# Token-ordered transposed blocks, a one-run load of block 0, an earlier W_out and a split last eviction in a convolution + GELU MLP kernel

## The chip, the cores and the metric

One core of one Trainium2 chip. The metric is the device time of one execution in microseconds (us); lower is better. The kernel before takes 686.33 us (median of 3 executions, 686.15 to 686.39). Inside a profile the clock starts with the span, so a profile's span (684.45 us for the kernel before) is about 1.8 us shorter than the time of the same execution. The pages print spans to 0.1 us; spans to 0.01 us are read from the kept traces. The profile is always that of one execution, the first (for the kernel before one of 686.27 us, which is not among the three); the other executions give only their time.

## The reference

A causal depthwise convolution with 7 taps over tokens (softmax over the taps, one weight row for each of 8 heads), then a two-layer MLP with exact GELU, on 8 x 4096 tokens of 192 values:

```python
w = softmax(weight, axis=-1)                       # [8 heads, 7 taps]
x_pad = concat([zeros(B, 6, 192), x], axis=1)
y[b, s, h, :] = sum_k w[h, k] * x_pad[b, s + k, h, :]
out = gelu(y.reshape(32768, 192) @ w_in) @ w_out   # w_in [192, 2048], w_out [2048, 192]
```

## The kernel before

The tokens are cut into two halves, which run side by side in the upper and the lower 64 partitions, and each half into 35 blocks: 6 of 256 tokens (0 to 5), then 29 of 512, of which the last (34) is evicted and stored in its own way. PE is TensorE, DVE is VectorE, ACT is ScalarE; SP, ACT and GpSimd issue the DMAs. For each block: DMA loads, three DVE transposes of 32x32 tiles (a column of `xT` is then a token), 7 taps on the DVE (blocks 0 and 1 on PE instead, with diagonal matrices), the first matmul (PE), GELU (ACT), the second matmul (PE), an eviction (a copy of the result out of `ob`, the PSUM tensor that the second matmul writes), stores. In the code shown, `...` marks a cut, and comments at the ends of lines are added.

The order of the tokens is set by the load. Partition `s` of a group of 32 takes `mb` *consecutive* tokens; after the transposes column `32*j + s` holds token `s*mb + j`:

```python
def load(e, n, qs=(0, 2, 1, 3), sm=None):
    mb = WS[n] // 32
    ...                                  # q: two halves of the tokens x two halves of the 192 values
        ap(xin[n % NX], 32*q*(TB//32*DQ), [[TB//32*DQ, 32], [DQ, mb], [1, DQ]]),
        ap(xt, off, [[mb * D, 32], [D, mb], [1, DQ]]),        # DQ = 96 values = 384 bytes
```

So a tap, one token back, is a shift by 32 columns, and the first 6*32 columns of each block (the halo) must be filled by GpSimd, mostly from the same block:

```python
src = ap(xT[n % 2], p * XW + 32 * kt, [[NP * XW, 128], [1, w]])      # a tap's source (DVE)
g.tensor_copy(ap(t, 1, [..., [32, HB], [1, 31]]),                    # 558 elements per partition
              ap(t, WS[n], [..., [32, HB], [1, 31]]))                # GpSimd, each block from 2 on
```

At the start GpSimd issues the W_in loads, then ten x loads of blocks 1 to 3 with W_out between them. SP and ACT each issue two of block 0's four loads; ACT does so *ahead of the Exp of the softmax*:

```python
load(a, 0, (2, 3))                 # ACT: two DMA issues
a.wait_ge(S_ACTP, 1)
a.wait_ge(S_PRO, 1)
a.activation(out=wex[:, :], in_=wsb[:, :], func=AF.Exp, ...)
```

At the end each 128x384 result of the last block is evicted by the DVE, and SP and ACT then issue two stores of 48 KB each.

## Time and profile before

| | before |
|---|---|
| time, median of 3 | 686.33 us |
| profile span | 684.45 us |
| busy PE / DVE / ACT / GpSimd | 677.3 / 580.5 / 532.6 / 46.0 us |
| first tap matmul of block 0 | 8.04 us |
| a 512-token block in the steady part | 20.72 us |
| last matmul to end of span | 3.40 us |

How to read it: PE is busy all the time and owns 96% of the chain of work that ended last. An engine with idle time may become faster and nothing happens.

### The profile page before, as it was taken

How to read it: one execution, taken by the hardware profiler on the slowest of the kernel's cores; microseconds unless marked ns; L12 is line 12 of the kernel's file. 1: busy time of each engine (PE TensorE's matmuls, PEld its weight loads, DVE VectorE, ACT ScalarE, POOL GpSimd, SP SyncE). 2: the span in 40 equal slices, each digit the busy share in tenths (PEclk: the TensorE clock that was granted, in tenths of full speed). 3: DMA queues.
4: the chain of work that ended last, by engine and by line, in shares of the span. 5: the costliest groups of instructions: out<-in, count | busy, mean ns of one | idle time of the engine just before them, and what ended most of it. 6: DMA issues, size and time to landing. Idle time of an engine off the chain costs nothing.

```text
span 684.5 us, 27314 instructions
## 1 busy us (share of the span) xinstructions
PE 677.3 (99%) x12548; PEld 409.0 (60%) x12548; DVE 580.5 (85%) x914; ACT 532.6 (78%) x536; POOL 46.0 (7%) x97
## 2 busy tenths in 40 slices
PE   8999999999999999999999999999999999999997
PEld 4899655555555555555555555555555555555556
DVE  7999999888899888898888898888898888998702
ACT  6788987877787777787877878777778777877771
POOL 8110000000000000000000000000000000000000
PEclk9999999999999999999999999999999999999999
DMA  8544531344432344422444422444322444221224
GB/s 135 95 107 99 117 61 32 64 94 95 94 67 50 76 94 95 93 52 55 85 94 95 88 51 53 95 94 95 72 54 66 95 94 95 61 53 31 48 49 94
DMA packets 133234, 53.66 MB, mean 78 GB/s; under 512 B 127552, under 2 KB 132960, under 8 KB 133120
## 3 DMA queue, kind: packets, MB, share of 16 engines
q1 hardware_dynamic: 128144, 48.78, 33.3%
q0 software_dynamic: 3792, 2.56, 2.4%
q8 instruction: 98, 1.61, 1.0%
q10 hardware_dynamic: 1184, 0.59, 0.3%
q14 instruction: 16, 0.13, 0.1%
HBM read 28.31 MB, written 25.17 MB: 78 GB/s over the span
## 4 chain that ended last, share of the span: by engine, by line
PE 96%; ACT 2%; DMA 1%; issue 0%; DVE 0%; SPq 0%
PE hp L683 47%; PE ob L747 42%; PE ob L714 6%; ACT gT L612 2%; PE ob L640 1%; DMA xin<-in_x_dram 1%; ACT osb L227 0%; DVE osb L247 0%; SPq L258 0%; DVE osb L229 0%; DVE xT L478 0%; ACT xTb L572 0%; SPq L795 0%; ACT xc L579 0%
## 5 line engine op out<-in xcount | busy, mean ns | idle before, releaser
L612 ACT ACTIVATE gT<-hp 128x1024 bf16<-128x1024 f32 x512 | 523.4, 1024 | 132.7 <-PE hp L683 129.6
L683 PE MATMUL hp<-xc,win 64*64 64x512 bf16 (+2 forms) x6048 | 418.5, 366 | 1.1 <-ACT gT L612 0.7
L747 PE MATMUL ob<-gT,wout 64*64 64x512 bf16 x5376 | 366.3, 376 | 0.0
L508 DVE SCALAR_TENSOR_TENSOR acc<-xT,wcol,acc 128x512 f32<-128x512 f32 (+1 forms) x495 | 314.0, 697 | 0.0
L683 PEld LDWEIGHTS hp<-xc,win 64*64 64x64 bf16 (+1 forms) x6048 | 187.7, 106 | 135.6 <-ACT gT L612 2.1
L747 PEld LDWEIGHTS ob<-gT,wout 64*64 64x64 bf16 x5376 | 172.1, 118 | 123.0
L247 DVE STREAM_TRANSPOSE osb<-ob 128x512 f32<-128x512 f32 x84 | 73.7, 880 | 86.8 <-PE ob L747 86.8
L478 DVE STREAM_TRANSPOSE xT<-xin 128x512 f32<-128x512 f32 (+1 forms) x105 | 78.5, 799 | 0.2 <-DMA xin<-in_x_dram 0.2
L508 DVE SCALAR_TENSOR_TENSOR xc<-xT,wcol,acc 128x512 bf16<-128x512 f32 (+1 forms) x99 | 65.1, 711 | 0.0
L374 POOL COPY xT<-xT 128x558 f32<-128x558 f32 x33 | 21.6, 654 | 578.6 <-DVE xT L478 578.6
L501 DVE TENSOR_SCALAR acc<-xT,wcol 128x512 f32<-128x512 f32 (+1 forms) x99 | 56.1, 618 | 1.1
L714 PE MATMUL ob<-wout,gT 64*128 64x192 bf16 x1024 | 52.2, 243 | 0.3
L714 PEld LDWEIGHTS ob<-wout,gT 64*128 64x128 bf16 x1024 | 43.5, 94 | 6.5 <-PE ob L714 0.6
L357 POOL COPY xT<-xT 128x18 f32<-128x18 f32 x30 | 11.6, 387 | 1.4 <-DVE xc L461 1.4
L229 DVE COPY osb<-ob 128x384 f32<-128x384 f32 x4 | 2.2, 557 | 7.8 <-PE ob L714 7.8
L625 PE MATMUL hp<-warm 128*128 128x512 bf16 x16 | 5.7, 533 | 1.3 <-DVE warm L394 1.3
L640 PE MATMUL ob<-xTb,dg 64*64 64x256 bf16 x84 | 5.3, 271 | 1.1 <-ACT xTb L572 1.1
L227 ACT ACTIVATE osb<-ob 128x384 f32<-128x384 f32 x12 | 5.8, 486 | 0.0
L258 POOL DMA_DIRECT2D xin<-in_x_dram x10 | 5.8, 588 | 0.0
L640 PEld LDWEIGHTS ob<-xTb,dg 64*64 64x64 bf16 x84 | 4.3, 106 | 2.2 <-ACT xTb L572 1.6
L625 PEld LDWEIGHTS hp<-warm 128*128 128x128 bf16 x16 | 2.0, 129 | 4.5 <-issue 2.7
L324 POOL DMA_DIRECT2D win<-in_moe_w_in_dram x6 | 3.9, 651 | 0.0
(32 smaller groups left out, 21.7 us busy)
## 6 DMA issues: line engine op xcount, KB each, us to landing
xin<-in_x_dram SPq DMA_DIRECT2D x116, 192.0 KB, 4.4
out_dram<-osb SPq DMA_DIRECT2D x112, 192.0 KB, 3.6
out_dram<-osb SPq DMA_DIRECT2D x56, 48.0 KB, 1.7
xin<-in_x_dram SPq DMA_DIRECT2D x12, 96.0 KB, 2.7
xin<-in_x_dram POOLq DMA_DIRECT2D x10, 96.0 KB, 2.7
wout<-in_moe_w_out_dram POOLq DMA_DIRECT2D x1, 768.0 KB, 8.6
win<-in_moe_w_in_dram POOLq DMA_DIRECT2D x4, 96.0 KB, 4.2
win<-in_moe_w_in_dram POOLq DMA_DIRECT2D x2, 192.0 KB, 5.3
```

The source lines that it names most:

```text
L247: v.transpose(ap(osb[m % 2], j, [[8 * C, 128], [C // 2, TB // 32], [NP, 32]]), bank(ring(m, j)),).then_inc(S_EV)
L357: g.tensor_copy(dst, ap(xT[(n - 1) % 2], WS[n - 1] + 31, [[NP * XW, 128], [XW, NP], [32, HB]],),).then_inc(S_HALO)
L374: g.tensor_copy(ap(t, 1, [[NP * tw, 128], [tw, NP], [32, HB], [1, 31]]), ap(t, WS[n], [[NP * tw, 128], [tw, NP], [32, HB], [1, 31]]),).the ...
L478: v.transpose(ap(xT[n % 2], p * XW + HL, [[NP * XW, 128], [1, w]]), ap(xin[n % NX], p, [[TB // 32 * DQ, 128], [DQ, w // 32], [NP, 32]],),) ...
L501: ins = v.tensor_scalar(a, src, wk, None, ALU.mult)
L508: ins = v.scalar_tensor_tensor(dst, src, wk, a, op0=ALU.mult, op1=ALU.add)
L612: a.activation(out=ap(gT[n % 2], i * c * 2 * w, dst), in_=ap(hp[u % 2], 0, src), func=AF.Gelu,).then_inc(S_GELU)
L625: t.matmul(hp[1][:, 0:512], warm[:, 0:128], warm[:, :])
L640: ins = t.matmul(bank(CONVB[n][p], r, w), dg[r, d0 : d0 + 64], xTb[PC[n]][r, x0 : x0 + w], start=(k == KS - 1), stop=(k == 0), tile_positi ...
L683: ins = t.matmul(hp[u % 2][fo : fo + fw, o : o + w], win[r, f1 : f1 + fw], xc[n % 2][r, p * TB : p * TB + w], start=(p == 0), stop=(p == N ...
L714: ins = t.matmul(bank(bb[sub], w=C), gT[m % 2][r, c0 : c0 + 128], wout[r, CH[i] * C : (CH[i] + 1) * C], start=(ph == 0 and i == 0), stop=( ...
L747: ins = t.matmul(bank(ring(m, j), slice(64 * h, 64 * h + 64), w), ap(wout, 64 * hf * NF * C + CH[i] * C + j, [[NF * C, 64], [NP, 64]],), g ...
```

## The change

Its intent: keep tokens in order, so that a tap is a shift by one column and the halo is 6 columns; save GpSimd's long copies; store in token order; load block 0 in one contiguous run per partition; issue W_out before the x loads of the later blocks; halve the last evictions, and store the last results with one larger DMA per queue instead of two. The core of the diff:

```diff
+    HX = 8
+    HF = HX - (KS - 1)
+    XW = HX + TB
...
+                if n == 0:
+                    dst = [[TB // 32 * DQ, 32], [1, mb * D - DQ]]      # one run of 1440 elements
+                    src = [[mb * D, 32], [1, mb * D - DQ]]
+                else:
+                    dst = [[TB // 32 * DQ, 32], [DQ, mb], [1, DQ]]
+                    src = [[D, 32], [32 * D, mb], [1, DQ]]             # tokens 32 apart
...
-                src = ap(xT[n % 2], p * XW + 32 * kt, [[NP * XW, 128], [1, w]])
+                src = ap(xT[n % 2], p * XW + HF + kt, [[NP * XW, 128], [1, w]])
...
             halo(0)
-            load(g, 1, SW[1], S_XG[1])
-            load(g, 2, SW[2], S_XG[2])
             g.dma_start(... wout ...)
             halo(1)
-            load(g, 3, SW[3], S_XG[3])
...
-            load(sp, 1, (0, 1))
-            sp.wait_ge(S_XG[3], 64)
+            load(sp, 1)
+            load(sp, 2)
+            sp.wait_ge(S_WOUT, 16)
+            load(sp, 3)
...
-                store_group(a, NB - 1, g, (2, 3))
+                evac_half(a, g, 1)            # ACT evicts one half, the DVE the other
+                store_half(a, g, 1)           # one store of 96 KB per queue
```

Block 0 alone keeps its old order, because there the one-run load delivers consecutive tokens.

More of the change, by code (lines that the diff above doesn't have):

```diff
@@ L42, in bass_lightweight_conv__then__act_gelu_exact_kernel @@
     assert NF == 16
+    HX = 8
+    HF = HX - (KS - 1)
+    XW = HX + TB
     HB = KS - 1
     HL = 32 * HB
-    XW = HL + TB
     XB = HL + WS[0]
@@ L82, in bass_lightweight_conv__then__act_gelu_exact_kernel @@
         CH += [2 * s, 2 * s + 1, NF // 2 + 2 * s, NF // 2 + 2 * s + 1]
-    PLAIN = [NCH[n] > 1 or n == NB - 1 for n in range(NB)]
     assert all(WS[n] == TB for n in range(M0, NB))
@@ L87, in bass_lightweight_conv__then__act_gelu_exact_kernel @@
     for n in range(NB):
-        OUTS.append((64 * NG[n] if PLAIN[n] else 64) + (OUTS[n - 2] if n >= 2 else 0))
+        k = 64 if n == 0 or M0 <= n < M1 else 16 * NG[n] if n < NB - 1 else 32 * NG[n]
+        OUTS.append(k * (NG[0] if n == 0 else 1) + (OUTS[n - 2] if n >= 2 else 0))
     es = ExitStack()
@@ L128, in bass_lightweight_conv__then__act_gelu_exact_kernel @@
         ob = pst("ob", [128, 2048])
-        SW = {1: (2, 3), 2: (0, 2, 1, 3), 3: (0, 2, 1, 3)}
         S_WSB = sem("S_WSB")
@@ L135, in bass_lightweight_conv__then__act_gelu_exact_kernel @@
         S_WOUT = sem("S_WOUT")
-        S_XG = {n: sem("S_XG%d" % n) for n in SW}
         S_XIN = [sem("S_XIN%d" % i) for i in range(NX)]
@@ L158, in bass_lightweight_conv__then__act_gelu_exact_kernel @@
         S_EVA = sem("S_EVA")
+        S_EVB = sem("S_EVB")
         block = es.enter_context(nc.Block())
@@ L183, in bass_lightweight_conv__then__act_gelu_exact_kernel @@
         for n in range(NB):
-            HC.append(HC[n] + (1 + NP if n in PC else 2))
+            HC.append(HC[n] + (1 + NP if n == 0 else 1))
         def wcols(hf, f):
@@ L190, in xin_at @@
         def xin_at(n):
-            return sum(64 - 16 * len(SW.get(m, ())) for m in range(n % NX, n + 1, NX))
+            return 64 * (n // NX + 1)
         def banks(m, g):
@@ L217, in wait_banks @@
                 t.wait_ge(S_EV, EVC[M1] + (-2 if e == 0 else e - 1))
+                if e >= 2:
+                    t.wait_ge(S_EVB, e - 1)
         def evac(e, m, g):
@@ L225, in evac, with evac_half, store_half @@
             src = ap(ob, 512 * b0, [[2048, 128], [512 * (b1 - b0), 2], [1, C]])
-            if m < NA:
-                e.activation(out=dst, in_=src, func=AF.Copy).then_inc(S_EVA)
-            else:
-                e.tensor_copy(dst, src).then_inc(S_EV)
+            e.activation(out=dst, in_=src, func=AF.Copy).then_inc(S_EVA)
+        def evac_half(e, g, h):
+            m = NB - 1
+            e.wait_ge(S_MM2, MMC[m] + g + 1)
+            if g == 0:
+                e.wait_ge(S_OUT[m % 2], OUTS[m - 2])
+            dst = osb[m % 2][:, (4 * h + g) * C : (4 * h + g + 1) * C]
+            src = bank(banks(m, g)[h], w=C)
+            if h == 0:
+                e.tensor_copy(dst, src).then_inc(S_EV)
+            else:
+                e.activation(out=dst, in_=src, func=AF.Copy).then_inc(S_EVB)
+        def store_half(e, g, h):
+            m = NB - 1
+            if h == 0:
+                wait_ev(e, m, g)
+            else:
+                e.wait_ge(S_EVB, g + 1)
+            e.dma_start(
+                ap(outt, (h * HALF + OFF[m] + 128 * g) * C, [[C, 128], [1, C]]),
+                osb[m % 2][:, (4 * h + g) * C : (4 * h + g + 1) * C],
+            ).then_inc(S_OUT[m % 2], 16)
         UPLO = [(1, 0), (0, 2), (2, 1)]
@@ L257, in load @@
                 off = ((q // 2) * HALF + OFF[n]) * D + DQ * (q % 2)
-                e.dma_start(
-                    ap(
-                        xin[n % NX],
-                        32 * q * (TB // 32 * DQ),
-                        [[TB // 32 * DQ, 32], [DQ, mb], [1, DQ]],
-                    ),
-                    ap(xt, off, [[mb * D, 32], [D, mb], [1, DQ]]),
-                ).then_inc(sm or S_XIN[n % NX], 16)
-        def store_group(e, m, g, qs=(0, 1, 2, 3)):
-            mb = WS[m] // 32
-            wait_ev(e, m, g)
-            for q in qs:
+                if n == 0:
+                    dst = [[TB // 32 * DQ, 32], [1, mb * D - DQ]]
+                    src = [[mb * D, 32], [1, mb * D - DQ]]
+                else:
+                    dst = [[TB // 32 * DQ, 32], [DQ, mb], [1, DQ]]
+                    src = [[D, 32], [32 * D, mb], [1, DQ]]
@@ new lines, in load, with store @@
+                e.dma_start(
+                    ap(xin[n % NX], 32 * q * (TB // 32 * DQ), dst), ap(xt, off, src)
+                ).then_inc(sm or S_XIN[n % NX], 16)
+        def store(e, m):
+            if m < M0:
+                for g in range(NG[m]):
+                    wait_ev(e, m, g)
+                    if m > 0:
+                        e.dma_start(
+                            ap(
+                                outt,
+                                (OFF[m] + 128 * g) * C,
+                                [[C, 128], [HALF * C, 2], [1, C]],
+                            ),
+                            ap(osb[m % 2], g * C, [[8 * C, 128], [4 * C, 2], [1, C]]),
+                        ).then_inc(S_OUT[m % 2], 16)
+                        continue
+                    mb = WS[m] // 32
+                    for q in range(4):
+                        e.dma_start(
+                            ap(
+                                outt,
+                                (OFF[m] + 4 * g + q) * C,
+                                [[mb * C, 32], [HALF * C, 2], [1, C]],
+                            ),
+                            ap(
+                                osb[m % 2],
+                                32 * q * 8 * C + g * C,
+                                [[8 * C, 32], [4 * C, 2], [1, C]],
+                            ),
+                        ).then_inc(S_OUT[m % 2], 16)
+                return
+            wait_ev(e, m, NP - 1)
+            for q in range(4):
@@ L274, in store_group @@
                         outt,
-                        (OFF[m] + 4 * g + q) * C,
-                        [[mb * C, 32], [HALF * C, 2], [1, C]],
+                        ((q // 2) * HALF + OFF[m]) * C + (q % 2) * (C // 2),
+                        [[C, 32], [32 * C, WS[m] // 32], [1, C // 2]],
                     ),
@@ L279, in store_group @@
                         osb[m % 2],
-                        32 * q * 8 * C + g * C,
-                        [[8 * C, 32], [4 * C, 2], [1, C]],
+                        32 * q * 8 * C,
+                        [[8 * C, 32], [C // 2, WS[m] // 32], [1, C // 2]],
                     ),
                 ).then_inc(S_OUT[m % 2], 16)
-        def store(e, m):
-            if PLAIN[m]:
-                for g in range(NG[m]):
-                    store_group(e, m, g)
-                return
-            j = NG[m]
-            mb = WS[m] // 32
-            wait_ev(e, m, EVC[m + 1] - EVC[m] - 1)
-            for q in range(4):
-                if M0 <= m < M1:
-                    dst = ap(
-                        outt,
-                        ((q // 2) * HALF + OFF[m]) * C + (q % 2) * (C // 2),
-                        [[mb * C, 32], [C, mb], [1, C // 2]],
-                    )
-                    src = ap(
-                        osb[m % 2],
-                        32 * q * 8 * C,
-                        [[8 * C, 32], [C // 2, mb], [1, C // 2]],
-                    )
-                else:
-                    dst = ap(
-                        outt,
-                        (OFF[m] + j * q) * C,
-                        [[mb * C, 32], [HALF * C, 2], [1, j * C]],
-                    )
-                    src = ap(
-                        osb[m % 2],
-                        32 * q * 8 * C,
-                        [[8 * C, 32], [4 * C, 2], [1, j * C]],
-                    )
-                e.dma_start(dst, src).then_inc(S_OUT[m % 2], 16)
         @block.gpsimd
@@ L344, in halo @@
             def halo(n):
-                t, tw = (xTb[PC[n]], XB) if n in PC else (xT[n % 2], XW)
-                dst = ap(t, 0, [[NP * tw, 128], [tw, NP], [32, HB]])
-                if n >= 2 and n not in PC:
+                if n == 0:
+                    t = xTb[0]
+                    g.memset(
+                        ap(t, 0, [[NP * XB, 128], [XB, NP], [32, HB]]), 0.0
+                    ).then_inc(S_HALO)
+                    for p in range(NP):
+                        g.wait_ge(S_TR, p + 1)
+                        g.tensor_copy(
+                            ap(t, p * XB + 1, [[NP * XB, 128], [32, HB], [1, 31]]),
+                            ap(
+                                xT[0],
+                                p * XW + HX + WS[0] - HL,
+                                [[NP * XW, 128], [32, HB], [1, 31]],
+                            ),
+                        ).then_inc(S_HALO)
+                    return
+                t, tw = (xTb[1], XB) if n in PC else (xT[n % 2], XW)
+                dst = ap(t, HF, [[NP * tw, 128], [tw, NP], [1, HB]])
+                if n >= 2:
                     if n - 2 in PC:
@@ L354, in halo @@
                     g.memset(dst, 0.0).then_inc(S_HALO)
-                else:
-                    g.wait_ge(S_TR, NP * n)
-                    g.tensor_copy(
-                        dst,
-                        ap(
-                            xT[(n - 1) % 2],
-                            WS[n - 1] + 31,
-                            [[NP * XW, 128], [XW, NP], [32, HB]],
-                        ),
-                    ).then_inc(S_HALO)
-                if n in PC:
-                    for p in range(NP):
-                        g.wait_ge(S_TR, NP * n + p + 1)
-                        g.tensor_copy(
-                            ap(t, p * tw + 1, [[NP * tw, 128], [32, HB], [1, 31]]),
-                            ap(xT[n % 2], p * XW + WS[n], [[NP * XW, 128], [32, HB], [1, 31]]),
-                        ).then_inc(S_HALO)
-                    return
-                g.wait_ge(S_TR, NP * (n + 1))
-                g.tensor_copy(
-                    ap(t, 1, [[NP * tw, 128], [tw, NP], [32, HB], [1, 31]]),
-                    ap(t, WS[n], [[NP * tw, 128], [tw, NP], [32, HB], [1, 31]]),
-                ).then_inc(S_HALO)
+                    return
+                g.wait_ge(S_TR, NP * n)
+                if n == 1:
+                    src = ap(
+                        xT[0],
+                        HX + WS[0] - HL + 31,
+                        [[NP * XW, 128], [XW, NP], [32, HB]],
+                    )
+                else:
+                    src = ap(
+                        xT[(n - 1) % 2],
+                        HF + WS[n - 1],
+                        [[NP * XW, 128], [XW, NP], [1, HB]],
+                    )
+                g.tensor_copy(dst, src).then_inc(S_HALO)
             g.wait_ge(S_IDN, 2)
             halo(0)
-            load(g, 1, SW[1], S_XG[1])
-            load(g, 2, SW[2], S_XG[2])
             g.dma_start(
@@ L454, in cast @@
                 v.tensor_copy(
-                    ap(xTb[PC[n]], p * XB + HL, [[NP * XB, 128], [1, WS[n]]]),
-                    ap(xT[n % 2], p * XW + HL, [[NP * XW, 128], [1, WS[n]]]),
+                    ap(xTb[PC[n]], p * XB + HX, [[NP * XB, 128], [1, WS[n]]]),
+                    ap(xT[n % 2], p * XW + HX, [[NP * XW, 128], [1, WS[n]]]),
                 ).then_inc(S_CAST[PC[n]])
@@ L469, in trans @@
                         v.wait_ge(S_XIN[n % NX], xin_at(n))
-                    if n in SW:
-                        v.wait_ge(S_XG[n], 16 * len(SW[n]))
                     if n >= 2 and n - 2 in PC:
@@ L478, in trans @@
                 v.transpose(
-                    ap(xT[n % 2], p * XW + HL, [[NP * XW, 128], [1, w]]),
+                    ap(xT[n % 2], p * XW + HX, [[NP * XW, 128], [1, w]]),
                     ap(
@@ L482, in trans @@
                         p,
-                        [[TB // 32 * DQ, 128], [DQ, w // 32], [NP, 32]],
+                        [[TB // 32 * DQ, 128], [D if n == 0 else DQ, w // 32], [NP, 32]],
                     ),
@@ L541, in _ @@
                 for g in range(NG[n]):
-                    side.append(((n + 3, g), evac, v, n, g))
+                    side.append(((n + 3, g), evac_half, v, g, 0))
             side.sort(key=lambda q: q[0])
@@ L573, in _ @@
                     out=ap(xTb[0], p * XB + HL, [[NP * XB, 128], [1, WS[0]]]),
-                    in_=ap(xT[0], p * XW + HL, [[NP * XW, 128], [1, WS[0]]]),
+                    in_=ap(xT[0], p * XW + HX, [[NP * XW, 128], [1, WS[0]]]),
                     func=AF.Copy,
@@ L603, in _ @@
                         dst = [[NF * 2 * TB, 128], [1, 2 * TB]]
-                    elif not PLAIN[n]:
-                        src = [[2 * TB, 128], [w // 4, 8], [32, w // 128], [1, 32]]
-                        dst = [[NF * 2 * TB, 128], [32, 8], [256, w // 128], [1, 32]]
                     else:
@@ L634, in pconv @@
                 if k == KS - 2:
-                    t.wait_ge(S_HALO, HC[n] + 2 + p)
+                    t.wait_ge(S_HALO, HC[n] + 2 + p if n == 0 else HC[n + 1])
                 for hf in range(2):
@@ L638, in pconv @@
                     d0 = (p * KS + k) * 64
-                    x0 = p * XB + 32 * k
+                    x0 = p * XB + (32 * k if n == 0 else HF + k)
                     ins = t.matmul(
@@ L804, in _ @@
             for g in range(NG[NB - 1]):
-                store_group(sp, NB - 1, g, (0, 1))
+                store_half(sp, g, 0)
             for s in range(2):
```

## The prediction

> **What bounds the kernel now.** I read the page first (busy time, the chain that ended last), then the chain in order of time, then the timelines of the three stretches that the change touches.
>
> ```profile
> PE 677.3 (99%) x12548; PEld 409.0 (60%) x12548; DVE 580.5 (85%) x914; ACT 532.6 (78%) x536; POOL 46.0 (7%) x97
> ...
> PE 96%; ACT 2%; DMA 1%; issue 0%; DVE 0%; SPq 0%
> PE hp L683 47%; PE ob L747 42%; PE ob L714 6%; ACT gT L612 2%; PE ob L640 1%; DMA xin<-in_x_dram 1%; ACT osb L227 0%; DVE osb L247 0%; SPq L258 0%; DVE osb L229 0%; DVE xT L478 0%; ACT xTb L572 0%; SPq L795 0%; ACT xc L579 0%
> ```
>
> The matmuls own 96% of the chain. In the chain in order of time the same piece (16 matmuls of L747) comes back at 143.74, 164.46, 185.18 us: a 512-token block takes 20.72 us. It holds 384 matmuls (192 on L683, 192 on L747), so 54.0 ns each; no wait stands between them. About 580 of the 684.5 us are 28 such blocks, and this change alters no matmul in them. What it can win lies before 90 us and after 670 us.
>
> The beginning, from the chain in order of time:
>
> ```profile
> 2.04 4.96 DMA xin<-in_x_dram
> 7.00 0.02 issue
> 7.03 0.53 DVE xT L478
> 7.55 0.02 issue
> 7.58 0.43 ACT xTb L572
> 8.00 0.04 issue
> 8.04 2.50 PE ob L640 x42
> ```
>
> After that come the GELUs of block 0 (11.66 to 14.64 us) and from 14.69 us on PE again, without a gap. The load of block 0 opens the chain, but only just: the DVE ended its diagonals at 6.84 us and sat idle 0.19 us before the first transpose.
>
> The end, from the timeline:
>
> ```profile
> 679.76 0.56 DVE L229 COPY osb<-ob 128x384 f32<-128x384 f32 x1 [3.40 <-PE ob L714]
> 679.80 1.24 PE L714 MATMUL ob<-wout,gT 64*128 64x192 bf16 x26
> ...
> 680.35 2.10 SPq L272 DMA_DIRECT2D out_dram<-osb  x4
> 680.35 2.18 ACTq L272 DMA_DIRECT2D out_dram<-osb  x4
> 681.08 0.56 DVE L229 COPY osb<-ob 128x384 f32<-128x384 f32 x1 [0.76 <-PE ob L714]
> ```
>
> The last matmul ends near 681.04, the last eviction at 681.64; SP and ACT then issue two stores each (the second ones at 682.0 and 682.1), and the span ends at 684.5: 3.46 us after PE.
>
> **Where DVE and GpSimd meet.** The first tap's 99 TENSOR_SCALARs on L501 take 335, 474 and 1031 ns at least, in the middle and at most. In a 256-token block:
>
> ```profile
> 28.82 1.35 DVE L501 TENSOR_SCALAR acc<-xT,wcol 128x256 f32<-128x256 f32 x3
> 30.09 6.01 DVE L508 SCALAR_TENSOR_TENSOR acc<-xT,wcol,acc 128x256 f32<-128x256 f32 x15
> ...
> 28.85 0.66 POOL L374 COPY xT<-xT 128x558 f32<-128x558 f32 x1 [8.36 <-DVE xT L478]
> 29.44 0.27 POOL L357 COPY xT<-xT 128x18 f32<-128x18 f32 x1
> ```
>
> The first TENSOR_SCALAR took 0.83 us (its own timeline), one left alone takes 0.335: GpSimd's halo copy of 558 elements costs the DVE about 0.5 us in every block.
>
> [...]
> [...]
> [...] From 256 to 512 elements L501 goes from 335 to 474 ns, 0.54 ns per element; L508 goes from 402 to 667 (busy over count), 1.04. [...]
> [...] Here 128144 packets of about 384 B on the SP and ACT ring's q1 took 33.3% of 16 engines' span: 0.333*684.5*16/128144 = 28.5 ns each, 13.4 GB/s per engine. [...]
> [...] The 48 KB stores of this trace land 1.7 us (median) after issue[...].
>
> **The change, part by part.**
>
> *Taps as a shift by one column.* From block 1 on, a partition of a load takes tokens 32 apart, so the transposed block is in token order. The 33 GpSimd copies of 558 elements (21.6 us busy) go, also 3 of the 6 casts L368; one 18-element halo copy per block stays (0.27 to 0.41 us). The DVE runs the same 693 tap operations of the same sizes. I expect 667 and 402 ns per L508 as now, since a run of consecutive columns stays one. The worst TENSOR_SCALAR should drop from 1031 towards 700 ns, because only the small copy is left to block it. That gives the DVE 0.2 to 0.5 us per block, say 0.3: 32 * 0.3 = 10 us of its 580.5. Value on the clock in the steady part: zero, since PE has no wait there (DVE 18.2 us busy per 20.7 us block). Around block 6 the DVE is nearest to binding: it ends block 6's taps at 72.88 us and PE starts on them at 73.55, slack 0.67 us. More slack there, but again no time.
>
> *Loads.* Pieces stay at 384 B, as many as before, only at 24 KB steps in DRAM instead of 768 B. Loads have a block and more to land. Zero.
>
> *Block 0's load.* One run of 8*192-96 = 1440 elements (5760 B) per partition instead of 8 pieces of 384 B: 128 pieces instead of 1024, but 737 KB instead of 393, as the other half of the model dimension comes along. Gain: at most the 0.19 us that the DVE idled. Cost: 344 KB more beside W_in. At the 176 to 188 GB/s that the stretch windows show from 3 to 7 us, that is up to 1.9 us of DMA time if nothing gets more efficient; larger pieces should win back part of it. Who pays? W_in's first part let SP go on at about 7.2 us and the DVE copies it at 8.89: 1.7 us of slack. Block 1's transposes start at 12.59 and its first PE tap at 15.44; the cast between ended at 14.24: 1.2 us of slack. I book 0, with a tail upward.
>
> *All loads of blocks 1 to 3 on SP, W_out first on GpSimd.* GpSimd's ten x issues (5.8 us) go; W_out is issued at about 9.07 instead of 12.49 us, and at its 8.6 us to landing arrives near 17.7 instead of 21.1. PE's weight loads waited 0.29 us for it at 21.11, PE itself about 0.02. Gain: 0 to 0.1 us. SP's four loads of block 1 start at 7.2, take 0.58 us each to issue, and the last, issued at 8.9, lands 3.5 us later at 12.4: just in time for 12.59. Without W_out's traffic ahead of it this should hold.
>
> *Stores in token order.* Blocks 1 to 5: 2 issues instead of 8 per block. SP was on time; zero. Blocks 6 to 30: as many and as large; zero.
>
> *The last block.* Each 128x384 eviction (557 ns on DVE) becomes 128x192 on DVE beside 128x192 on ACT. At 1.04 ns per element[...] the DVE half takes 557-200 = 357 ns; ACT's ran 384 elements in 486 and 256 in 384, so about 335. Gain 0.2 us. Each queue then issues one store instead of two: the second issue came 0.4 us after the first. The larger one takes perhaps 0.1 us longer to issue. Gain 0.3. Sum 0.5 us, all of it on the path, as nothing lies beside the end.
>
> Sum: 0.5 (end) + 0.1 (W_out and start) = 0.6 us. 686.33 - 0.6 = **685.7 us**.
>
> **Rivals.**
> *A: the DVE taps slow down at odd columns.* A 512-token block costs the DVE 18.9 us of 20.72: 21 taps (3 at 585, 15 at 667, 3 at 690 ns, busy over count) give 13.83, six transposes (3 at 809, 3 at 877) give 5.06. So 1.8 us are spare and it takes 13% slower taps to bind. At 20%: 2.77 - 1.8 = 0.97 us, times 25 blocks, 24 us: 710. For it: the offsets are no longer multiples of 128 B. Against it: nothing in the profile[...], and 0.3 us come back from GpSimd. In blocks 2 to 6 (16.8 to 72.9 us, DVE without a gap) 0.67 + 5*0.3 = 2.2 us are spare, so 4% slower taps would bind there and cost little.
> *B: block 0's larger load or the shared SP queue delays the start.* If x(0) lands 1 us late the whole kernel ends 0.8 to 1 us later: 686.5 to 687. For it: 344 KB more in the busiest 5 us of the DMA engines. Against it: piece count down eightfold.
> *C: the spare DVE time turns into speed.* That needs PE waits for DVE; after the warm-up the list of waits has none longer than 0.4 us. It would make 685.5 at best.
> *D: the 24 KB strides make loads or stores slower.* Loads land after 4.4 us and stores after 3.6; they would have to take over 10 us more to stall a 20.7 us block. 686 at worst.
>
> **Range and chances.** The sum gives 685.7. The end is firm within 0.3 us; the start may add up to 1.5 (B, about one in five) or give 0.2 more. So 684.9 to 687.1 for 8 in 10. Two per cent is 13.7 us, or 0.55 us in each of 25 blocks; only A at 17% or more ((1.8 + 0.55)/13.83) reaches that: 2%. Faster by 2% would need work taken from PE, and there is none: 1%. Same 97%.
>
> **What would show it.** Right: PE's block period still 20.72 us; L374 gone, L501's maximum under 750 ns, DVE busy near 570 us; L508 within 2% of 667 ns; last PE matmul to end of span near 3.0 us instead of 3.46; first transpose at 6.9 to 7.1 us. Wrong: a first transpose after 7.5 us or PE idle for block 1's taps at 15.4 us (B); longer L508 with PE waiting on DVE (A); or PE's period changed, which nothing here explains.

The sum is 0.2 (halved eviction) + 0.3 (one store per queue) + 0.1 (W_out and start) = 0.6 us, and 686.33 - 0.6 = 685.7. In it, 1.04 ns per element is what L508 shows; that the eviction copy would follow it was an estimate (measured: 557 ns for 384 elements, 358 for 192), and "perhaps 0.1 us longer to issue" was the author's guess (measured: 0.37 us for ACT's 96 KB store after, 0.45 for a 48 KB one before, medians). "Larger pieces should win back part of it" has this measured beside it: in the first 9 us ACT's queue moved 0.37 MB in 15.0% of the engines' time after, and 0.20 MB in 9.4% before, so 24.7 against 21.3 KB for each 1%.

## More of the kernel before

Only two stretches have no full PE: the beginning (block 0 must be loaded, transposed and convolved first) and the end (the last result must leave).

## The result

The changed kernel took 685.25 us (median of 4: 684.97, 685.22, 685.28, 686.65) against 686.24 us of before (685.98 to 686.39, 4 executions). The ratio is 0.999, 95% interval 0.9973 to 1.0007: the same. A ratio is the mean time of one kernel's runs over the mean of the other's of the same rounds, so it is not quite the ratio of the medians quoted. The predicted 685.7 with 684.9 to 687.1 holds it.

The page after (busy time, then the chain that ended last by engine):

```profile
PE 676.7 (99%) x12548; PEld 411.2 (60%) x12548; DVE 564.3 (83%) x914; ACT 534.0 (78%) x540; POOL 20.4 (3%) x51
...
PE 96%; ACT 2%; DVE 1%; issue 0%; DMA 0%; ACTq 0%
```

The DVE lost 16.2 us and GpSimd 25.6 us of work, and the chain is still PE's at 96%. In the chain's list the DMA's 1% has become the DVE's: that is the start. The chain of the first microseconds after (start, duration, what):

```profile
2.46 0.40 ACT wex L585 x2
...
5.33 1.16 DVE dg L453 x2
6.50 0.44 DVE xT L501
6.93 0.02 issue
6.96 0.42 ACT xTb L595
7.38 0.04 issue
7.42 2.48 PE ob L660 x42
```

PE's first tap comes at 7.42 instead of 8.04 us. Before, the chain began with block 0's DMA. Now it begins with the softmax of the tap weights: Exp, small DVE steps, the diagonals (`dg`), and the transposes follow at once. The timeline of ACT shows why the softmax itself came earlier. Before:

```profile
1.24 1.34 ACTq L258 DMA_DIRECT2D xin<-in_x_dram  x2
...
2.69 0.30 ACT L562 ACTIVATE wex<-wsb,wmx 8x7 f32<-8x7 f32 x1 [0.39 <-DVE wmx L398]
```

and after:

```profile
1.25 0.89 ACTq L288 DMA_DIRECT2D xin<-in_x_dram  x2
...
2.46 0.30 ACT L585 ACTIVATE wex<-wsb,wmx 8x7 f32<-8x7 f32 x1 [0.15 <-DVE wmx L423]
```

ACT's two load issues take 0.89 us instead of 1.34: each has 32 pieces instead of 256, and in x0_pieces below, with 256 again, they take 1.34. The Exp stands behind them in the same queue: it starts 0.23 us earlier. (A piece is one contiguous run of bytes of a DMA.) A small DVE step of the softmax (`wnm`) also took 0.22 instead of 0.33 us, and the diagonals end at 6.49 instead of 6.84. Why that step varies was not found: it took 0.22 us in tail_only too, where the load is in pieces.

The end after, from the timeline:

```profile
680.42 0.33 ACT L241 ACTIVATE osb<-ob 128x192 f32<-128x192 f32 x1 [0.99 <-PE ob L734]
680.42 0.36 DVE L239 COPY osb<-ob 128x192 f32<-128x192 f32 x1 [0.96 <-PE ob L734]
680.78 0.37 ACTq L249 DMA_DIRECT2D out_dram<-osb  x1
```

The last matmul ends at 680.40 and the span at 683.23: 2.83 us instead of 3.40. Between the two ends nothing moved: 680.40 - 7.42 = 672.98 us, against 681.05 - 8.04 = 673.01 before, and a block still takes 20.72 us (157.12 to 177.84 in the chain). So in the profiles 0.62 us came from the start and 0.57 from the end.

One new wait stands in the list of waits after:

```profile
DVE xT L501 <- DMA xin<-in_x_dram: 0.9, 1, 0.9
```

That is block 2's transpose at 17.15 us. Its load was issued from about 9 us and now shares the DMA engines with W_out, which landed 10.3 us after its issue instead of 8.6. Here nothing waited for the DVE because of it.

### The profile page after: what moved, and what is told of

Read it like the earlier page. It is cut to its first block, busy times and chain, and to the rows that moved or that the text cites. A ratio compares the mean times of both kernels' runs of the same rounds, so it can differ in the third digit from the quotient of the medians.

```text
span 683.2 us, 27246 instructions
## 1 busy us (share of the span) xinstructions
PE 676.7 (99%) x12548; PEld 411.2 (60%) x12548; DVE 564.3 (83%) x914; ACT 534.0 (78%) x540; POOL 20.4 (3%) x51
## 4 chain that ended last, share of the span: by engine, by line
PE 96%; ACT 2%; DVE 1%; issue 0%; DMA 0%; ACTq 0%
PE hp L703 48%; PE ob L767 42%; PE ob L734 5%; ACT gT L631 2%; PE ob L660 1%; DMA wsb<-in_weight_dram 0%; DVE dg L453 0%; ACT osb L228 0%; DVE wcol L445 0%; DVE osb L270 0%; DVE xT L501 0%; ACT xTb L595 0%; ACT wex L585 0%; DVE osb L239 0%; DVE wch L439 0%
## 5 line engine op out<-in xcount | busy, mean ns | idle before, releaser
L524 DVE TENSOR_SCALAR acc<-xT,wcol 128x512 f32<-128x512 f32 (+1 forms) x99 | 40.7, 467 | 1.1
L239 DVE COPY osb<-ob 128x192 f32<-128x192 f32 x4 | 1.4, 358 | 8.4 <-PE ob L734 8.4
L464 DVE COPY win<-win 64x768 bf16<-64x768 bf16 (+1 forms) x6 | 3.7, 620 | 0.2
## 6 DMA issues: line engine op xcount, KB each, us to landing
wout<-in_moe_w_out_dram POOLq DMA_DIRECT2D x1, 768.0 KB, 10.3
```

The source lines that it names most:

```text
L524: ins = v.tensor_scalar(a, src, wk, None, ALU.mult)
```

## The experiments

Twelve kernels ran, all five rounds (at most one execution lost), in three batches, each on one chip (the third on another chip than the first two) with the kernel before beside it: 686.42 in the first batch (9 executions), 686.55 (10, the first batch's nine among them) and 686.38 (9). All gave correct results. The table is the key to all of them. It takes the profiled execution apart into start (time of the first tap matmul) and rest (span minus start), and sets the median time beside them. "In pieces" is the load of block 0 in 384-byte pieces, as in the kernel before.

| run | what it is | first tap | span | rest | median of all executions |
|---|---|---|---|---|---|
| before | | 8.04 | 684.45 | 676.41 | 686.24 |
| after | | 7.42 | 683.23 | 675.81 | 685.25 |
| after_again | after, once more | 7.39 | 683.19 | 675.80 | 685.32 |
| order_only | token order alone | 7.79 | 684.15 | 676.36 | 686.06 |
| order_tail | token order + new end | 8.26 | 684.15 | 675.89 | 685.85 |
| x0_pieces | after, block 0 in pieces | 8.16 | 683.96 | 675.80 | 685.41 |
| pieces_whole | x0_pieces, evictions whole | 8.20 | 684.14 | 675.94 | 685.93 |
| wout_late | after, old issue order of W_out and the loads | 7.37 | 683.17 | 675.80 | 685.30 |
| exp_late | after, Exp held back | 7.46 | 683.28 | 675.82 | 685.20 |
| pool_copy | x0_pieces + wasted GpSimd copies | 7.78 | 683.59 | 675.81 | 685.89 |
| pieces_evac_dve | x0_pieces + 3 evictions on DVE | 7.95 | 684.03 | 676.08 | 685.89 |
| start_padded | after + 3.3 us idle work | 10.67 | 687.82 | 677.15 | 689.96 |
| tail_only | before + new end (failed) | 7.97 | 688.04 | 680.07 | 689.60 |
| before_evac_dve | before + 3 evictions on DVE | 9.25 | 686.58 | 677.33 | 688.18 |

Two things stand out. The rest takes only two values where nothing was spoilt: 676.36 to 676.41 with the old end, 675.80 to 675.94 with the new. And the start varies, from execution to execution too.

### after_again

No edit. 

> The changed kernel once more, for a well-sampled time beside the others. Theory (the gain lies at the two ends alone: about 0.6 us at the start, because block 0's load is issued faster, and 0.6 us at the end, because the last eviction and its stores are halved): 1.0 to 1.3 us under the kernel before in every pair. Rival (one of the four earlier runs, 686.65, shows that the gain is within the spread): no difference that five rounds can tell from zero.

Measured: 685.01, 687.52, 686.40, 685.32, 685.13 us, median 685.32, ratio 0.9992 (0.9978 to 1.0005). The median gain, 1.1 us, came again; but two of five executions lie more than 1.3 us over the fastest, and the interval includes 1. Neither side is fully right: the profile's gain is real in the fast executions, the mean gain is about half of it. This opened a second question, where that spread comes from. It is not the changed kernel's alone: the nine executions of the kernel before in this batch spread over 1.3 us (685.98 to 687.26).

### x0_pieces

```diff
                 if n == 0:
-                    dst = [[TB // 32 * DQ, 32], [1, mb * D - DQ]]
-                    src = [[mb * D, 32], [1, mb * D - DQ]]
+                    dst = [[TB // 32 * DQ, 32], [DQ, mb], [1, DQ]]
+                    src = [[mb * D, 32], [D, mb], [1, DQ]]
```

> The changed kernel with block 0's load back in 384-byte pieces. Theory: the whole gain at the start goes: the ACT queue's two load issues take 1.3 us again instead of 0.9, the Exp starts near 2.7 instead of 2.46 us, the first transpose near 7.0 instead of 6.4, the first tap matmul near 8.0 instead of 7.4; the time is 0.5 to 0.7 us over the changed kernel's. Rival (the early W_out, or the missing x issues of GpSimd, made the start faster): the first tap matmul stays near 7.4 us and the time stays.

In the profile the theory held. ACT's issues took 1.34 us again, the Exp started at 2.69 us, the diagonals ended at 6.85, and then the DVE waited for the load (timeline):

```profile
7.14 1.33 DVE L501 STREAM_TRANSPOSE xT<-xin 128x256 f32<-128x256 f32 x3 [0.29 <-DMA xin<-in_x_dram]
...
8.16 2.48 PE L660 MATMUL ob<-xTb,dg 64*64 64x256 bf16 x42 [1.22 <-ACT xTb L595]
```

The first tap came 0.74 us later than in the changed kernel, and the rest was the same. So in the profile the whole start gain hangs on block 0's load, and W_out and the missing GpSimd issues have no part in it. But the median time was 685.41, only 0.1 us over the changed kernel's, where 0.5 to 0.7 was expected; its profiled execution was the slowest of its five (685.33 to 685.79). The profile caught a late landing. In order_only and pool_copy, which load block 0 in the same pieces, the transposes started at 6.78 and 6.76 us with no wait at all, and PE at 7.79 and 7.78. So the faster issue is worth about 0.37 us (7.79 - 7.42) where the load lands in time, and the landing adds 0 to 0.4 us in these profiles. Over all executions little of this is left: the 18 of the four kernels with the one-run load (after, after_again, wout_late, exp_late) have a mean of 685.64 us, the 20 of the four with pieces and the new end (x0_pieces, order_tail, pieces_whole, pool_copy) 685.78. The medians differ by 0.5 us (685.29 and 685.76), the means by 0.14, which these spreads can't tell from zero.

### tail_only (a failed experiment)

The kernel before with the new end. Its results are not in token order, so the single store per queue got a destination of 4 x 32 rows:

```diff
+            e.dma_start(
+                ap(outt, (h * HALF + OFF[m] + 4 * g) * C, [[C, 4], [16 * C, 32], [1, C]]),
+                osb[m % 2][:, (4 * h + g) * C : (4 * h + g + 1) * C],
```

> The kernel before with the changed end alone: the last block's evictions halved between DVE and ACT, one store of 96 KB per queue and group. Theory: last matmul to end of span 2.8 us instead of 3.5; time 0.6 us under before. Rival (the end is set by the landing of the same 196 KB, whoever issues them): 3.3 us or more, time within 0.2 us of before.

Measured 689.60 us, ratio 1.0048: slower by 3.2 us, with 7.11 us instead of 2.8 from the last matmul to the end. The mistake is the store. DMA traffic of its last 12 us in 40 slices (busy share of the 16 engines in tenths, then GB/s):

```profile
DMA  9888882212222222222222222222222222221000
GB/s 180 172 173 173 175 144 24 20 45 77 90 79 90 95 92 92 92 77 95 92 95 90 95 92 92 84 95 90 95 92 95 72 92 92 92 90 59 13 0 0
```

and of the changed kernel's last 5.2 us:

```profile
DMA  0000000000000000017999700000799971000000
GB/s 6 0 0 0 0 0 12 6 12 12 6 0 0 0 0 0 0 35 260 343 319 325 213 18 0 0 0 6 248 343 331 313 237 36 0 0 0 0 0 0
```

The same 96 KB stores run at about 92 GB/s with two tenths of the engines busy, instead of 313 to 343 GB/s with nine. From 681.4 to 686.5 us the engines' mean busy share is 0.27, as much as 0.27 x 16 = 4.3 engines busy all the time. Why so few are busy was not shown; what differs in the store is its destination, 4 x 32 rows instead of 128 in one dimension. Together with order_tail, whose store of 128 rows lets the span end 2.83 us after the last matmul, the run shows that token order is a precondition of the cheap store, since only then are the 128 rows one dimension. It says nothing on the end's worth; order_tail repaired it.

Its profile does bear on the start, as here ACT's two issues happened to take longer still:

```profile
1.25 1.65 ACTq L285 DMA_DIRECT2D xin<-in_x_dram  x2
3.00 0.30 ACT L589 ACTIVATE wex<-wsb,wmx 8x7 f32<-8x7 f32 x1 [0.69 <-DVE wmx L425]
6.96 1.33 DVE L505 STREAM_TRANSPOSE xT<-xin 128x256 f32<-128x256 f32 x3
```

The Exp started at 3.00 us, the diagonals ended at 7.04, the load was not waited for, and the first tap came at 7.97. So with issues of 0.89, 1.34 and 1.65 us (after, order_only, tail_only) the Exp starts at 2.46, 2.69 and 3.00 us and the first tap comes at 7.42, 7.79 and 7.97: the start follows ACT's issues.

### order_only

The changed kernel with block 0 in pieces, the old end (whole evictions, two stores per queue, but in token order) and the old issue order of W_out and the loads. The edit is the sum of those of x0_pieces, wout_late and:

```diff
-                evac_half(a, g, 1)
-                store_half(a, g, 1)
+                store_q(a, g, (2, 3))     # two stores of 48 KB; the DVE evicts 128x384
```

> The changed kernel with block 0's load in pieces, the old end and the old issue order of W_out and the loads: what is left is the token order, so taps at odd columns and the small halo copy. Theory: the largest tensor_scalar of the first tap falls from 1031 to under 500 ns and the DVE is some 15 us less busy, while the time stays within 0.2 us of before. Rival C of the prediction (spare DVE time turns into speed): 0.3 us or more faster than before. Rival A (odd columns are slower): scalar_tensor_tensor over 680 ns per 512 columns.

Measured 686.06 us (685.96 to 686.49), ratio 0.9996 (0.9983 to 1.0008), 0.36 under before. The table tells that this is not spare DVE time: the rest is 676.36 against 676.41, and the first tap was 0.25 us earlier because this execution's load had landed in time. DVE taps of 512 columns cost 290.5/435 = 668 ns, 667 before: taps at odd columns cost nothing here. The DVE saved its 15 us, and the time did not follow. Rivals A and C of the prediction are out.

### order_tail

order_only with the halved end. 

> The token-order kernel with the old loads (block 0 in pieces, W_out late), plus the halved end; it repairs the run tail_only, whose single store had only 4 rows in its slowest dimension. Theory (the end is worth 0.6 us by itself): last matmul to end of span 2.8 us, time about 0.6 us under order_only (686.06), so 685.4, the same as with block 0 in pieces and W_out early (685.41), which would leave 0 for the early W_out. Rival (the early W_out carried part of the gain): 685.7 or more.

The profile: last matmul at 681.32, end of span at 684.15, so 2.83 us against order_only's 3.39, and a rest of 675.89 against 676.36. The end is worth 0.5 to 0.6 us by itself. x0_pieces differs from it only by the early W_out and the issue order of the loads, and its rest is 0.09 less, so these are worth 0.1 at most (wout_late below puts it at 0). In the times it is less clear: 685.85 (685.41 to 686.71), 0.2 under order_only, and in this execution the first tap was at 8.26 us, after a late landing (0.39 us of waiting). The expected 685.4 was met by two of five.

### pieces_whole

```diff
-                    side.append(((n + 3, g), evac_half, v, g, 0))
+                    side.append(((n + 3, g), evac_dve, v, n, g))   # one 128x384 copy
...
-                evac_half(a, g, 1)
                 store_half(a, g, 1)                                 # both wait for the DVE
```

> The changed kernel with block 0 in pieces, where the last block's evictions stay whole on the DVE but each queue issues one 96 KB store per group. It splits the end's 0.64 us. Theory: the halved eviction carries 0.2 (557 against 358 ns) and the saved second store issue 0.4, so this run lies 0.2 us over 685.41, with 3.0 us from the last matmul to the end. Rival (the eviction is most of it): 0.4 us or more over.

Last matmul 681.17, end 684.14: 2.97 us, against 2.83 (x0_pieces and after), and 3.39 to 3.40 with the old end. So the single store per queue carries about 0.43 of the 0.57 us and the halved eviction about 0.14, although its duration falls by 0.20 us (558 to 358 ns): near what was expected. The median, 685.93, cannot resolve this.

### wout_late

After, with the loads of blocks 1 to 3 split between SP and GpSimd and W_out issued behind those of blocks 1 and 2, as before. 

> The changed kernel (block 0 in one run per partition) with the loads of blocks 1 to 3 shared with GpSimd and W_out issued late, as before. The changed kernel's five runs spread over 2.5 us (685.01 to 687.52), those with block 0 in pieces over 0.5. Theory S1 (the bigger load of block 0 by itself makes some executions start late, as it competes with W_in): the spread stays, with some runs above 686.3. Theory S2 (the early W_out and SP's loads collide with it): the spread goes and all runs lie near 685.1.

Four executions: 685.00, 685.29, 685.30, 686.72. The slow execution is still there, so the early W_out is not its only cause (S2 falls as the whole cause). The rest is 675.80 against 675.81: the issue order is worth nothing in the time. Block 2's transpose came at 16.11 us without a wait here (nor did it wait in order_only and order_tail), against 0.9 us of waiting in the changed kernel (0.3 to 1.8 in the other unpadded profiles with W_out ahead).

### exp_late

```diff
             load(a, 0, (2, 3))
+            a.activation(out=dum[:, :], in_=warm[:, 0:256], func=AF.Copy)
             a.wait_ge(S_ACTP, 1)
```

> The changed kernel with one small copy on ACT between its load issues and the Exp, to hold the softmax chain back as the longer issues of the kernel before did. Theory (the Exp waits behind ACT's load issues, and this opens the chain): the Exp starts near 2.7 us, the diagonals end near 6.8 instead of 6.5 and the first tap matmul comes near 7.75 instead of 7.4: 0.3 to 0.4 us lost in the profile. Rival (the load's landing at about 6.4 us sets the start): the first transpose moves by less than 0.1 us. If slow executions come from a late landing, their times should not rise with the delay while the fast ones do.

Inconclusive, because the delay came out too small: ACT would have waited for the weights' load anyway until 2.36 us, and the copy held the Exp back by only 0.11 us (2.52 against 2.41 in after_again). The diagonals, the transposes and the first tap each came 0.06 to 0.07 us later. That points the way of the theory but falls under the 0.1 us that the rival allowed. The Exp's part rests on x0_pieces, order_only, pool_copy and the start of tail_only instead.

### start_padded

```diff
             diag(1)
+            for d in range(5):
+                v.scalar_tensor_tensor(dmb_[d][:, :], dma_[:, :], wcol[:, 0:1], dma_[:, :], ...)
             for p in range(NP):
                 trans(0, p)
```

> The changed kernel with five idle DVE operations (3.3 us) ahead of block 0's transposes, so that block 0, W_in and W_out have all landed before they are needed. The time rises by about 3.3 us. The four kernels with the one-run load of block 0 have shown 6 of 18 executions 1.0 to 2.5 us over their fastest. Theory S1 (the landing of the loads in the first 12 us varies from execution to execution): the spread goes, all five times lie within 0.4 us. Rival S3 (the spread comes from elsewhere, the steady part or the end): one or two of the five again lie more than 1 us over the fastest.

Five times: 689.76, 689.96, 689.77, 690.05, 690.01. The spread of 0.29 us replaces one of 1.3 to 2.5, which points to the start, as S1 says. It does not exclude S3: where 6 of 18 executions are slow, five fast ones in a row still come by chance about one time in eight ((12/18)^5 = 0.13), and this batch ran on another chip. The rise was 4.6 us instead of 3.3, though. In stretches of the profile (the last three figures are the granted PE clock, the DMA share and GB/s):

```profile
11.00:12.00 1.00, 1.00 (x22) 1.00 (x20) 0.94 (x3) 0.77 (x3) 0.96 (x2) 1.00 1.12 246
12.00:13.00 1.00, 1.00 (x14) 0.85 (x11) 1.00 (x1) 0.39 (x2) 1.00 (x2) 0.50 0.65 142
```

PE's warm-up matmuls ended at 6.81 us and its next work came at 10.67; after that pause of 3.86 us the clock was granted at half from 12 to about 15.4 us. After pauses of 1.14 us (6.28 to 7.42, in after) and 1.85 us (7.40 to 9.25, in before_evac_dve) it stayed at 1.00. So the half clock is a side effect that the padding brought in; that the pause causes it was not tested, and it began only 1.3 us after PE had work again. (In tail_only, too, the clock fell: from 681.4 to 686.5 us, after the last matmul at 680.93, its mean was 0.65.) 3.4 us at half speed cost about 1.7 us of PE's work, enough for the 1.34 us by which the rest is longer than after's.

### pool_copy

```diff
                 halo(n)
+                g.wait_ge(S_TR, NP * (n + 1))
+                g.tensor_copy(dum, 558 elements of xT[n % 2]).then_inc(S_HALO)
```

> The changed kernel with block 0 in pieces (685.41) and a 558-element GpSimd copy per block put back at the old place, as waste. Theory[...]: the largest tensor_scalar goes from 489 back to about 1000 ns, DVE busy up by 14 to 16 us, and the time stays within 0.2 us. Rival (the tensor_scalar became faster through the new column pitch): it stays under 500 ns. Rival C (spare DVE time is speed): the time rises by 0.5 us or more.

The source view of the first tap's line gives duration in ns, min/median/max. Before, after, and with the wasted copy:

```profile
L501 DVE TENSOR_SCALAR acc<-xT,wcol x99: 335/474/1031, 18.4 to 629.6; 128x512 f32<-128x512 f32 x87, 128x256 f32<-128x256 f32 x12
```

```profile
L524 DVE TENSOR_SCALAR acc<-xT,wcol x99: 346/481/489, 18.7 to 628.5; 128x512 f32<-128x512 f32 x87, 128x256 f32<-128x256 f32 x12
```

```profile
L530 DVE TENSOR_SCALAR acc<-xT,wcol x99: 336/475/1014, 18.6 to 629.3; 128x512 f32<-128x512 f32 x87, 128x256 f32<-128x256 f32 x12
```

The long copy alone brings back the 1014 ns, and DVE busy time from 564 to 579.6 us; the column pitch has nothing to do with it. What the copy and the tensor_scalar contend for was not shown, nor whether the copy's length or the order of the two makes the difference. The rest of the execution is 675.81 us against 675.80 without it: 15 us of DVE work, and no change in the time. The median (685.89) is 0.5 over x0_pieces of another batch and chip, but level with order_tail and pieces_whole; by the rest, rival C is out here too.

### pieces_evac_dve and before_evac_dve

The question was whether the freed DVE time could buy anything. From 72 to 83 us ACT is on the chain, and it also evicts. Three of its evictions go to the DVE:

```diff
+            side += [((7, 6), evac_v, v, 4, 1), ((7, 18), evac_v, v, 5, 0), ((8, 6), evac_v, v, 5, 1)]
```

> The changed kernel with block 0 in pieces, and three evictions (the last of block 4, both of block 5; 0.48 us each on ACT) moved from ACT to the DVE, where ACT is the bound, 72 to 83 us. It asks what the freed DVE time could buy. Theory: the DVE ends the taps of block 6 some 2.4 us and of block 7 some 3 us ahead of PE, takes the 3 times 0.56 us, and PE gains 0.4 to 0.7 us: about 684.9 against 685.41. Rival (PE is as full as ACT there): within 0.2 us.

> The same three evictions moved to the DVE in the kernel before. There the DVE ends block 6's and block 7's taps only 0.7 us ahead of PE. Theory: the two evictions that come ahead of block 7's last tap cost it 1.1 us, PE now waits for the taps of block 7 and gives back what it won: within 0.3 us of before or slower. Rival (the freed DVE time is not needed for this): the same gain as on the changed kernel, 0.4 to 0.7 us.

Block 6 did get shorter on the changed kernel. The stretch from its first matmul to block 7's, in after and in pieces_evac_dve (length, then busy PE, PE loads, DVE, ACT):

```profile
72.89:89.00 16.11, 15.98 (x232) 9.44 (x232) 16.07 (x26) 16.11 (x19) 0.89 (x2) 1.00 0.34 76
```

```profile
74.16:89.80 15.64, 15.64 (x229) 9.32 (x228) 15.61 (x26) 15.36 (x17) 0.45 (x1) 1.00 0.34 78
```

That is 0.47 us, as expected. But the same profile lost 0.6 us in block 1, which its chain shows:

```profile
10.69 7.85 DMA xin<-in_x_dram
18.55 0.02 issue
18.57 1.33 DVE xT L511 x3
...
20.65 0.43 DVE xc L496
21.08 0.05 issue
21.13 0.61 PE hp L715 x8
```

Block 2's load took 7.85 us to land, with W_out (issued at 8.92 us) in flight. The DVE stood 1.80 us in front of block 2's transpose; behind it in its program are the evictions of block 1's taps (`xc`), and PE waited for those. It is the new wait of the changed kernel, twice as long as in its own profile. The median is 685.89 (685.24 to 686.23), no better than its base, so no version that beats the changed kernel was shown.

On the kernel before, the move cost time: 688.18 (686.91 to 688.56), ratio 1.0018 (1.0004 to 1.0032). In its profile the taps of blocks 6 and 7 stand on the chain (DVE, most of 70.7 to 91.1 us). The run is not clean, as this execution's first load was also late:

```profile
8.23 1.33 DVE L488 STREAM_TRANSPOSE xT<-xin 128x256 f32<-128x256 f32 x3 [1.40 <-DMA xin<-in_x_dram]
```

The two fast executions (686.91 and 686.98) still lie 0.5 us over before's median, and from the first tap to the last matmul the profile took 673.42 us against 673.01. So in the kernel before the DVE had no time to give there, and in the changed one it has. This line also shows how late block 0's load can be: 1.40 us of waiting, against none in order_only.

## Why the prediction was right or wrong

The total was right (0.6 us predicted; 1.0 and 1.1 measured in the medians, 1.2 in the profiles, 0.7 and 0.6 in the means, all inside the range), but one of its two terms, the start, was far too small, because one step was wrong. That the means come so near to the 0.6 is luck: the fast executions gained twice that, and slow ones gave it back.

**The steady part.** Right. Block period 20.72 us, no matmul and no wait of PE changed, taps at 290.9/435 = 669 ns against 667. Taps at odd columns cost nothing here. The DVE fell to 564.3 us instead of "near 570" and the longest TENSOR_SCALAR to 489 ns instead of "towards 700": no TENSOR_SCALAR is delayed by the small copy that is left (median 481 ns).

**The end.** Right in mechanism and nearly in size: 0.5 predicted, 0.57 measured (3.40 to 2.83; the prediction's 3.46 comes from a span rounded up to 684.5). In the split, the halved eviction gave about 0.14 (predicted 0.2) and one store per queue about 0.43 (predicted 0.3).

**Block 0's load.** The failed step is "Gain: at most the 0.19 us that the DVE idled". It held the end of the diagonals fixed at 6.84 us. But the load's shape also sets how long the issuing queue is occupied (ACT's two issues: 1.34 us in pieces, 0.89 in one run), ACT's queue holds the Exp, and the Exp opens the chain to the diagonals. Both ends of the comparison moved: the diagonals to 6.49 us and the landing to before 6.41, where the first transpose began (forecast: 6.9 to 7.1). Term of the sum: 0.1 predicted for W_out and start together, 0.62 in the profiles (0.35 by the diagonals, the rest by the landing). x0_pieces shows that it all comes from this load. It holds for executions in which the load lands in time; in the means it is not resolved.

**The tail upward (rival B).** Named with one chance in five, and it is there, without being the load's alone. Of 18 executions of the four kernels with the one-run load and an unpadded start, 6 lie 1.2 to 2.5 us over the fastest; of 20 with pieces and a single store per queue (x0_pieces, order_tail, pieces_whole, pool_copy), 3 lie over 686.4. The kernel before has such a spread too (1.3 us in nine executions). start_padded points to the start. Two ways were seen in profiles: block 0's load landing up to 1.4 us after the DVE is ready (in pieces, on the kernel before; the same load was in time in order_only, pool_copy and tail_only, and kept the DVE waiting 0.19, 0.29, 0.32, 0.39 and 1.40 us in five other profiles), and block 2's load behind W_out. Which of them a slow execution of the changed kernel has was not seen, since only first executions are profiled, and those of this kernel were all fast. A half-speed PE after a long pause, as in the padded kernel, is not it: the mean granted clock is 1.0 in all six slow ones, and 0.997 or 0.998 in the five padded ones. What makes those executions slow stays open.

**W_out.** Right that it is worth nothing: PE's 0.02 us wait was all it could remove. It landed at 8.40 + 10.3 = 18.7 us, not 17.7. Wrong in "Loads have a block and more to land. Zero.": block 2's load does not have it, the DVE waited 0.9 us in the profile after, and 1.8 us in another execution reached PE.

**Rivals A, C, D.** (Two slips in the prediction's readings change nothing: it gives the DVE's work per block as 18.2 us and, in rival A, as 18.9 from a sum over groups; busy time says 18.2 (438.6 us in 500), so 2.5 us were spare and not 1.8. And queue q1 is SP's alone, ACT's is q10: before, q10 carries 0.59 MB, which is ACT's two loads of 96 KB and eight stores of 48 KB.) A fell (668 and 669 ns). C fell (order_only and pool_copy: 15 us of DVE work, no time). D fell: loads land after 4.0 us (4.4 before) and 192 KB stores after 3.1 (3.6).

## What to carry to other kernels

Split every profile at the first useful matmul: start and rest answer different questions, and here the rest repeats to about 0.1 us while the start varies by more than the whole gain. A DMA's shape has a price at its issuer (here 1.34 against 0.89 us for two loads), so ask what stands behind the issue in the same queue, above all in a prologue, and do not hold one leg of a join fixed while you shorten the other. Time freed on an engine that is not the bound was worth nothing here (15 us of DVE work, 0.05 us of the rest) until something was moved onto it (0.47 us in block 6), and moving a transfer ahead moved another one back (W_out ahead, and the DVE waited 0.9 us for block 2's load).
